# Sixteen identity products ahead of each whole K pair's first products, layers 0 and 1

## Chip, cores and metric

One core of a Trainium2 chip runs the kernel. The metric is the device time of one execution in microseconds (us); lower is better. Figures called "span" run from the first to the last instruction of one execution that was profiled.

## What is computed

Four attention layers for one token follow each other, with the weights and caches A, B, A, B. The part that matters:

```python
def _A_ref(x, k_cache, v_cache, wq, wo):          # _B_ref is the same with its own weights
    q = (x @ wq).reshape(B, Sq, Hq, Dh).transpose(0, 2, 1, 3)     # Sq = 1, Hq = 32, Dh = 192
    scores = jnp.einsum("bhqd,bhkd->bhqk", q, k) * (Dh ** -0.5)   # 8192 keys per head
    p = _softmax(scores, axis=-1)
    o = jnp.einsum("bhqk,bhkd->bhqd", p, v)
    return o.transpose(0, 2, 1, 3).reshape(B, Sq, Hq * Dh) @ wo

x = x + _A_ref(_layernorm(x), A_k_cache, A_v_cache, A_wq, A_wo)
x = x + _B_ref(_layernorm(x), B_k_cache, B_v_cache, B_wq, B_wo)
# and both once more
```

All tensors are bf16. One head's keys are 8192 x 192, so the K of two heads is 6.29 MB (6144 KB) and their V as much again. Each layer reads all 32 heads.

## The kernel before

**Tiling.** A layer works on 16 pairs of heads. K and V of a pair lie on 128 partitions with 64 partitions for each head and 128 keys on each partition. The buffer `pool` in SBUF has eight slots of 128 x 12288 bf16; one slot holds one half of a pair's keys (a "unit", 64 keys on each partition), two neighbouring slots hold a whole pair.

**Scores of a pair.** `products` (from line 725) does one unit. VectorE multiplies the K in place by the query, which is laid out as a row on every partition (line 737), in pieces along the 192 head elements: 96, 64 and 32 for the pairs that this change concerns. TensorE then adds up over the head elements: 24 products of 128 x 512 with the identity as weights accumulate in one PSUM bank of `S` (line 752 for the first, which loads the weights, and the helper at line 72 for those that keep them). Each piece is waited for by itself: 12, 8 and 4 products follow the three pieces. A second unit goes to the other bank. After both, VectorE reduces `S` to scores (line 792), `softmax` follows, and `values` (lines 822 and 849) multiplies the probabilities by V on TensorE. `gather` has VectorE collect the output (lines 873 and 875), and TensorE and ScalarE bring it into a row (lines 887 and 896). After pairs 4 and 9 the output projection of five pairs follows on TensorE (lines 715 and 688).

**Order.** The list `steps` gives the order in which every engine's instructions are written; an engine takes its own in that order. For a pair p in the middle of a layer it reads: products of one unit, products of the other, softmax, values, gather, then the same of pair p + 1. So on TensorE the products of pair p + 1 stand behind the line 887 product of pair p.

**Loads.** The list `plan` gives the order of the loads; SyncE issues them all (line 473 for K and V pairs), and each waits until its slots are free (`before`, `freed`). K's slots are free when the identity products of their unit are done, V's slots when `values` is done. In layers 0 and 1 the pairs 1 to 13 (those in `KPOS`) are loaded whole, as one transfer of 6.29 MB for K and one for V. V always goes to slots 0 and 1. K alternates between slots 2 and 3 and slots 3 and 4, so K of pair p + 1 shares one slot with K of pair p: it can be issued when the first unit of pair p is done, and `units` puts the shared slot's unit first. From pair 4 to 5 and from 9 to 10 K stays in the same two slots and waits for both units. In layers 2 and 3 the slots are handed out more freely.

**The helper `busy`** issues products of the identity with the identity, 128 x 512, into the first bank of `S`; nobody reads them. They wait until the last reduction of `S` has read that bank. The kernel uses it with 16 products at the end of layers 1 and 3, and with one to six in four other places, none of them in the middle of a layer.

Of the kernel before, what the change touches and what calls it, by code (L numbers as in the profile page):

```python
# [82 lines left out]
def build(nc, A_x, A_k, A_v, A_wq, A_wo, B_x, B_k, B_v, B_wq, B_wo, out):  # L83
# [31 lines left out]
    with ExitStack() as ctx:  # L115
# [18 lines left out]
        KPOS = {}  # L134
# [101 lines left out]
        def first_load(kind, l, p):  # L236

            n = (kind, pair(l, p))
            if l >= 2 and n in KEPT[l - 2]:
                return (l - 2, ORDER[l - 2]["pairs"].index(n[1]))  # L240
            return (l, p)
# [4 lines left out]
        def units(l, p):  # L246

            return (1, 0) if l < 2 and p in KPOS and KPOS[p] == RING else (0, 1)
# [11 lines left out]
        steps, plan, joint = [], [], set()  # L260

        def both(*ns):
            plan.extend(ns)
            steps.extend(ns)

        for l in range(NL):
            if l < 3:
                plan += [("wq", l, 0), ("wq", l, 2)][:(1, 2, 0)[l]]
                ahead_of = [{0: (0, DC)}, {0: (0, DC - 1), 2: (DC - 1, DC)}, {0: (0, 1), 2: (1, DC)}][l]
                for c in ([0, 2, 3, 1, 4] if l == 2 else range(DC)):  # L270
                    steps += [("lead", l, 0, *ahead_of[c])] if c in ahead_of else []
                    steps.append(("r", l, c))
            else:
                both(("wq", l, 0))
            for p in range(NPAIR):
                if l == 0 and p == 0:
                    plan.append(("kh", l, p))
                if l == 2 and p == 0:
                    plan += [("kp", l, p, i) for i in range(1, len(PIECE))]
                else:  # L280
                    plan += [("k", l, p, u) for u in range(2)]
                if l == 2 and p == 0:
                    steps.append(("mq", l, p, 0))
                    for i in range(1, 4):
                        steps += [("mq", l, p, i), ("rd", l, p, i - 1)]
                    steps.append(("rd", l, p, 3))
                else:
                    steps.append(("m", l, p, units(l, p)[0]))
                    if l == 2 and p == 1:
                        steps.append(("e", l, 0))  # L290
                    steps.append(("m", l, p, units(l, p)[1]))
                if p == NPAIR - 1:
                    steps.append(("v", l, p - 1))
                steps.append(("s", l, p))
                if l == 3 and p == 0:
                    both(("wq", l, 1), ("wq", l, 2))
                if p < NPAIR - 2:
                    if first_load("v", l, p) == (l, p):
                        plan += [("v", l, p, u) for u in range(2)]
                    steps.append(("v", l, p))  # L300
                    if l != 2 or p > 0:
                        steps.append(("e", l, p))
                    if p + 1 in (PAIRS_W, 2 * PAIRS_W):
                        b = (p + 1) // PAIRS_W - 1
                        steps.append(("wc", l, b))
                        both(("wo", l, b))
            for i in (p - 1, p):
                if first_load("v", l, i) == (l, i):
                    plan += [("v", l, i, u) for u in range(2)]
            plan.insert(-1 if l < 2 else -2, ("wo", l, 2))  # L310
            steps += [("busy", l, 16), ("e", l, p - 1)] if NB[l] else [("e", l, p - 1)]
            steps += [("v", l, p, 0), ("wc", l, 2)] if NB[l] else [("wc", l, 2), ("v", l, p, 0)]
            steps += [("wo", l, 2), ("v", l, p, 1), ("e", l, p)]
            if NB[l]:
                plan.append(("vq", l))
                for i in range(len(WB[l])):
                    both(("wob", l, i))
            both(("wol", l))
            if l == 3:
                both(("woe", l))  # L320
# [662 lines left out]
def bass_interleave_layers__gqa_block_cached__mha_block_cached__decode_kernel(  # L983
    nc: bass.Bass,
    A_x: bass.AP,
    A_k_cache: bass.AP,
    A_v_cache: bass.AP,
    A_wq: bass.AP,
    A_wo: bass.AP,
    B_x: bass.AP,  # L990
    B_k_cache: bass.AP,
    B_v_cache: bass.AP,
    B_wq: bass.AP,
    B_wo: bass.AP,
    out: bass.AP,
):
    build(nc, A_x, A_k_cache, A_v_cache, A_wq, A_wo, B_x, B_k_cache, B_v_cache, B_wq, B_wo, out)
# [28 lines left out]
```

## Time and profile before

| what | figure |
|---|---|
| three runs | median 1992.69 us, 1990.37 to 1992.9 |
| the profiled execution | 1993.62 us, of which the span is 1991.7 us |
| mean granted TensorE clock | 0.791 of full speed |
| busy in the span | TensorE 1274.9 us (64%), VectorE 1201.3 us (60%), ScalarE 168.5 us (8%) |
| moved by DMA | 845.99 MB, mean 425 GB/s |
| identity products over K, line 72 | x3004, 787.1 us busy, 425 ns mean |
| identity products over K, line 752 (first of a group) | x66, 38.1 us busy, idle before them 236.4 us, all of it waiting for VectorE's line 737 |
| VectorE line 737 | x408, 841.1 us busy |
| products of `busy`, lines 526 and 72 | x6 and x37, 2.7 and 8.6 us busy |
| one K pair of A from issue to landing (13 whole ones) | median 19.2 us |

"Idle before" is the time in which the engine stood still just ahead of such instructions. A product's own duration contains the way through the array, so products in a row start closer together than their durations say. The granted clock is given as a share of full speed.

### The profile page before, as it was taken

The page shows a single profiled execution, that of the slowest core. Times are in us where ns is not written, and L with a number is a line of the kernel's source. Part 1 is how long each engine was busy: PE and PEld are TensorE (multiplying, and loading weights), DVE is VectorE, ACT ScalarE, POOL GpSimd, SP SyncE. Part 2 cuts the span into 40 slices and gives each one's busy share as a digit, 9 for nine tenths or more (in the row PEclk, how much of TensorE's full clock was granted, in tenths as well). Part 3 has the DMA queues.
Part 4 walks back from the last instruction along what each step waited for, and adds up shares of the span by engine and source line. Part 5 has one row for each costly group of instructions (what it writes and reads, how often), then busy time and mean ns, then how long its engine had stood idle before and what let it go on. Part 6 is the DMA issues. An engine that isn't in the chain of part 4 may idle for free.

```text
span 1991.7 us, 12071 instructions
## 1 busy us (share of the span) xinstructions
PE 1274.9 (64%) x7747; PEld 128.0 (6%) x2611; DVE 1201.3 (60%) x858; ACT 168.5 (8%) x529; POOL 4.6 (0%) x25
## 2 busy tenths in 40 slices
PE   4475665657565656656686666666666667657558
PEld 0000000000100000010010000000002001000001
DVE  3565574667256655656756755756773666765656
ACT  1000000000100000000000000000000100000000
POOL 0000000000000000000000000000000000000000
PEclk9777777778776877777888778877787788778779
DMA  9999999999999999999999999999999999999998
GB/s 411 434 417 417 423 423 428 402 427 428 429 432 414 427 423 401 423 425 427 429 416 432 432 429 432 434 427 429 439 423 426 436 435 433 429 435 432 430 435 368
DMA packets 27240, 845.99 MB, mean 425 GB/s; under 512 B 3122, under 2 KB 3252, under 8 KB 4148
## 3 DMA queue, kind: packets, MB, share of 16 engines
q1 hardware_dynamic: 27044, 845.23, 99.3%
q8 instruction: 40, 0.66, 0.1%
q14 instruction: 12, 0.10, 0.0%
q10 hardware_dynamic: 144, 0.00, 0.0%
HBM read 845.22 MB, written 0.00 MB: 424 GB/s over the span
## 4 chain that ended last, share of the span: by engine, by line
DMA 60%; PE 22%; DVE 16%; ACT 1%; issue 0%; SPq 0%; POOL 0%; ACTq 0%
DMA pool<-in_B_k_cache_dram 26%; DMA pool<-in_A_k_cache_dram 18%; PE S L72 15%; DMA pool<-in_A_v_cache_dram 14%; DVE pool L737 13%; PE OY L72 3%; PE OY L849 2%; DMA pool<-in_B_wo_dram 2%; DVE OY L873 1%; DVE acc L875 1%; PE S L752 1%; DMA pool<-in_B_v_cache_dram 1%; DVE s_sb L792 1%; DVE pool L766 1%; ACT p_sb L807 0%
## 5 line engine op out<-in xcount | busy, mean ns | idle before, releaser
L737 DVE TENSOR_TENSOR pool<-pool,q_sb 128x3072 bf16<-128x3072 bf16 (+4 forms) x408 | 841.1, 2129 | 181.0 <-DMA pool<-in_B_k_cache_dram 98.3
L72 PE MATMUL S<-pool,ident 128*128 128x512 bf16 x3004 | 787.1, 425 | 15.8 <-DVE pool L737 13.7
L873 DVE TENSOR_TENSOR OY<-OY,small 128x1536 f32<-128x1536 f32 x60 | 106.0, 1767 | 247.5 <-PE OY L72 247.3
L72 PE MATMUL OY<-pool,p_sb 128*16 128x512 bf16 x1920 | 206.8, 519 | 0.0
L752 PE MATMUL S<-pool,ident 128*128 128x512 bf16 x66 | 38.1, 577 | 236.4 <-DVE pool L737 236.4
L887 PE MATMUL TB<-acc,small 128*33 128x192 f32 x120 | 43.9, 461 | 207.0 <-DVE acc L875 207.0
L849 PE MATMUL OY<-pool,p_sb 128*16 128x512 bf16 (+1 forms) x1216 | 144.1, 497 | 44.3 <-DMA pool<-in_A_v_cache_dram 36.2
L792 DVE TENSOR_REDUCE s_sb<-S 128x128 f32<-128x1024 f32 x63 | 77.2, 1225 | 150.5 <-PE S L72 150.5
L587 ACT ACTIVATE q_sb<-QM 64x192 bf16<-64x192 f32 x118 | 38.4, 325 | 952.5 <-PE QM L640 951.9
L875 DVE TENSOR_REDUCE acc<-OY 128x192 f32<-128x1536 f32 x60 | 105.5, 1758 | 2.0
L896 ACT ACTIVATE rows<-TB,small 1x192 bf16<-1x192 f32 x120 | 49.5, 413 | 568.8 <-PE TB L887 567.3
L807 ACT ACTIVATE p_sb<-s_sb,small 64x128 bf16<-64x128 f32 x128 | 55.7, 435 | 172.7 <-DVE small L801 171.9
L797 PE MATMUL QM<-ident,m_bf 128*64 128x64 bf16 x128 | 14.1, 217 | 82.5 <-DVE m_bf L794 82.5
L863 DVE RECIPROCAL small<-TB 33x2 f32<-33x2 f32 x64 | 11.2, 175 | 89.7 <-PE TB L822 73.3
L822 PE MATMUL TB<-small,ones 128*33 128x2 f32 x120 | 14.6, 192 | 74.1 <-ACT p_sb L807 74.1
L640 PEld LDWEIGHTS QM<-rows,one_b 1*128 1x128 bf16 x59 | 5.4, 91 | 727.8 <-issue 727.8
L849 PEld LDWEIGHTS OY<-pool,p_sb 128*16 128x16 bf16 (+1 forms) x1216 | 35.3, 107 | 195.2 <-issue 141.7
L688 PE MATMUL OY<-pool,oT 128*1 128x320 bf16 x330 | 39.0, 414 | 2.4 <-ACT oT L718 2.2
L801 DVE TENSOR_REDUCE small<-QM 128x1 f32<-128x64 f32 x64 | 14.4, 225 | 33.2 <-PE QM L797 33.2
L887 PEld LDWEIGHTS TB<-acc,small 128*33 128x33 f32 x120 | 9.9, 128 | 306.9 <-DVE acc L875 306.9
L752 PEld LDWEIGHTS S<-pool,ident 128*128 128x128 bf16 x66 | 6.8, 103 | 273.5 <-DVE pool L737 272.4
L807 ACT ACTIVATION_READ_ACCUMULATOR p_sb<-s_sb,small 64x1 f32 x128 | 23.3, 182 | 0.0
(87 smaller groups left out, 248.5 us busy)
## 6 DMA issues: line engine op xcount, KB each, us to landing
pool<-in_B_v_cache_dram SPq DMA_DIRECT2D x28, 6144.0 KB, 27.4
pool<-in_A_v_cache_dram SPq DMA_DIRECT2D x27, 6144.0 KB, 24.0
pool<-in_B_k_cache_dram SPq DMA_DIRECT2D x27, 6144.0 KB, 21.4
pool<-in_A_k_cache_dram SPq DMA_DIRECT2D x35, 3072.0 KB, 19.9
pool<-in_A_k_cache_dram SPq DMA_DIRECT2D x13, 6144.0 KB, 19.2
pool<-in_A_v_cache_dram SPq DMA_DIRECT2D x10, 3072.0 KB, 14.3
pool<-in_B_k_cache_dram SPq DMA_DIRECT2D x10, 3072.0 KB, 18.7
pool<-in_A_wo_dram SPq DMA_DIRECT2D x6, 2400.0 KB, 18.3
```

The source lines that it names most:

```text
L72: return t.add_instruction(mybir.InstMatmult(name=t.bass.get_next_instruction_name(), engine=mybir.EngineType.PE, ins=[t.lower_ap(rhs), t. ...
L587: lambda a, h=h, r=r, f=f: a.activation(q_sb[i][r, :], QM[r, h * DH:(h + 1) * DH], ACT.Copy, scale=f),
L688: e = PE.op(lambda t, i=i, h=h, f=l < 3 and n[2] == 0 and i == 0, fin=n == last_row and i == k - 1: t.matmul(YR[32 * h:32 * h + 1, :], lhs ...
L737: e = DV.op(lambda v, d0=d0, QD=QD, kin=kin, kout=kout, n=n: v.tensor_tensor(kout[:, :, d0:d0 + QD], kin[:, :, d0:d0 + QD], q_sb[qi][:, d0 ...
L752: t.matmul(S[:, :], lhsT=ident[:], rhs=k3[:, :, d0:d0 + R], start=d0 == 0, stop=fin)),
L792: lambda v: v.tensor_reduce(s[:], S_[:].rearrange("p (j r) -> p j r", r=R), AX.X, ALU.add),
L807: ev_p[p] = AC.op(lambda a, h=h, r=r: a.activation(p_sb[par][r, :, h], s[r, :], ACT.Exp, bias=negm[par][r, 0:1], accum_out=l_col[par][r, h ...
L849: t.matmul(o, lhsT=x, rhs=y, start=f, stop=fin) if c == 0 else
L873: e = DV.op(lambda v: v.tensor_tensor(o3, o3, pick[:, 0:VK].unsqueeze(2).broadcast_to([P, VK, DH]), ALU.mult), bank=Ou)
L875: e = DV.op(lambda v: v.tensor_reduce(acc[:], O.rearrange("p (i d) -> p d i", d=DH), AX.X, ALU.add), e, bank=Ou)
L887: e = PE.op(lambda t: t.matmul(TB[64:97, C_O:C_O + DH], lhsT=half33, rhs=acc[:], start=True, stop=True), bank=TBu)
L896: last["TO"] = last["row_written"] = AC.op(lambda a, h=h: a.activation(orow[:, o0 + h * DH:o0 + (h + 1) * DH], TB[64 + 32 * h:65 + 32 * h, ...
```

## The change

For each of the pairs 1 to 13 in layers 0 and 1, the step `("busy", l, 16)` is written just ahead of the products of the pair's first unit.

```diff
@@ -285,6 +285,8 @@
                         steps += [("mq", l, p, i), ("rd", l, p, i - 1)]
                     steps.append(("rd", l, p, 3))
                 else:
+                    if l < 2 and p in KPOS:
+                        steps.append(("busy", l, 16))
                     steps.append(("m", l, p, units(l, p)[0]))
                     if l == 2 and p == 1:
                         steps.append(("e", l, 0))
```

The step calls this function, which is unchanged:

```python
        def busy(n):

            PE.wait(ev_const, last["S"][0])
            for i in range(n):
                PE.op(lambda t, i=i: (
                    t.matmul(SP_[0][:, :], lhsT=ident[:], rhs=ident[:].unsqueeze(1).broadcast_to([P, 4, P]), start=True, stop=True)
                    if i == 0 else
                    matmul_held(t, SP_[0][:, :], ident[:], ident[:].unsqueeze(1).broadcast_to([P, 4, P]), True, True)),
                    signal=False, bank=Su[0])
```

## The prediction

> **What bounds the kernel now.** I began with the page's forty slices: how busy the DMA engines are, what they move, and TensorE's clock.
>
> ```profile
> PEclk9777777778776877777888778877787788778779
> GB/s 411 434 417 417 423 423 428 402 427 428 429 432 414 427 423 401 423 425 427 429 416 432 432 429 432 434 427 429 439 423 426 436 435 433 429 435 432 430 435 368
> ```
>
> The transfers run all the time, but the first half of the span has slices of 401 to 417 GB/s, the second nearly none. The table by stage says how much that is. Its rows are two stretches of layers 0 and 1 (from the landing of K of pair 1 to that of pair 13), then one of layer 2 and one of layer 3. The last three columns are granted clock, busy share of the DMA engines and GB/s.
>
> ```profile
> 66.96:437.86 370.90, 229.87 (x1326) 18.81 (x378) 224.88 (x144) 29.84 (x98) 0.00 (x0) 0.76 0.99 419
> 580.48:952.11 371.63, 229.50 (x1346) 20.41 (x398) 224.89 (x144) 30.27 (x99) 0.00 (x0) 0.77 0.99 421
> 1093.88:1500.00 406.12, 268.05 (x1477) 20.36 (x403) 259.91 (x191) 32.31 (x106) 0.00 (x0) 0.79 1.00 431
> 1560.00:1940.00 380.00, 245.68 (x1461) 21.69 (x434) 242.97 (x142) 32.52 (x107) 0.00 (x0) 0.78 1.00 432
> ```
>
> No engine but DMA is near full, so the kernel is bound by its loads, and layers 0 and 1 load some 2.6% below the pace that layers 2 and 3 hold. At 432 GB/s a pair (12.58 MB) takes 29.13 us, and the twelve pairs with two output weights of 2.46 MB (5.69 us each) take 12 x 29.13 + 2 x 5.69 = 360.9 us. The rows have 370.9 and 371.6: **20.7 us** in all are lost there.
>
> The chain of waits, in order of time (start, length, what), shows where. First comes a pair with a short turn, then one with a long one.
>
> ```profile
> 251.76 3.37 DVE pool L737
> 255.78 6.09 PE S L72 x23
> 261.89 19.17 DMA pool<-in_A_k_cache_dram
> ...
> 347.87 3.37 DVE pool L737
> 351.89 7.51 PE S L72 x23
> 359.43 19.22 DMA pool<-in_A_k_cache_dram
> ```
>
> K lands, VectorE multiplies its first piece, TensorE sums up the first unit, and only then is the next K issued: 10.1 us after the landing in one pair, 11.6 us in the other. Read off in the same way for all pairs, the 20 that free the next K with their first unit fall into groups: seven issue it 10.1 to 10.4 us after the landing, and the next K lands 29.08 to 29.66 us after this one (mean 29.37); eleven issue it after 11.2 to 11.6 us, and the next lands 29.47 to 31.07 us after (mean 30.30); two lie between, at 29.06 and 29.48. A later issue makes a longer period, some 0.8 us for each us, and the shortest period is that of the bytes. At the late issues the transfers run dry: V of the pair takes 14.6 us at that pace behind its K, whose data ends before the landing is reported.
>
> Why is TensorE early or late? Its first product starts 3.41 us after the landing in all 26 pairs, when VectorE has the first piece; and in all 26 the granted clock at that moment is 0.50. It rises during the unit, sooner or later. The two stretches by time of the products of `S` alone, from pair 6 (after length, sum and the three engines: granted clock):
>
> ```profile
> 226.00:230.00 4.00, 4.00 (x11) 0.00 (x0) 0.00 (x0) 0.50 0.91 393
> 231.00:235.00 4.00, 4.00 (x20) 0.00 (x0) 0.00 (x0) 1.00 1.06 406
> ```
>
> Each stretch is 4 us: some ten products at half clock, some twenty at full, or 0.43 and 0.215 us each.
>
> **The change part by part.** It removes nothing and moves no transfer in SyncE's order. It adds 26 x 16 = 416 products and 26 weight loads on TensorE. The nearest row is the use at the end of layer 1 (the first product with its weight load, then 15):
>
> ```profile
> 1013.27 0.39 PE L526 MATMUL S<-ident 128*128 128x512 bf16 x1
> ...
> 1013.50 3.40 PE L72 MATMUL S<-ident 128*128 128x512 bf16 x15
> ```
>
> That is 3.63 us at full clock, and by the 0.43 us above 16 x 0.43 = 6.9 us at half. In TensorE's order they stand behind the line 887 product of the pair before. How long before the landing of K that ends decides everything. An early pair and a late one:
>
> ```profile
> 375.65 0.51 PE L887 MATMUL TB<-acc,small 128*33 128x192 f32 x2 [3.66 <-DVE acc L875]
> 378.67 13.30 DVE L737 TENSOR_TENSOR pool<-pool,q_sb 128x6144 bf16<-128x6144 bf16 x6 [3.07 <-DMA pool<-in_A_k_cache_dram]
> 382.08 0.61 PE L752 MATMUL S<-pool,ident 128*128 128x512 bf16 x1 [5.92 <-DVE pool L737]
> ```
>
> ```profile
> 251.00 0.80 PE L887 MATMUL TB<-acc,small 128*33 128x192 f32 x2 [3.65 <-DVE acc L875]
> 251.76 12.17 DVE L737 TENSOR_TENSOR pool<-pool,q_sb 128x6144 bf16<-128x6144 bf16 x5 [0.82 <-DMA pool<-in_A_k_cache_dram]
> 255.18 0.61 PE L752 MATMUL S<-pool,ident 128*128 128x512 bf16 x1 [3.37 <-DVE pool L737]
> ```
>
> In the first, TensorE idles for 5.92 us up to its first product, in the second for 3.4. Of the 26 pairs, 18 are early (TensorE free 1.3 to 6.1 us before the landing), 8 late (1.0 us before to 0.12 after). What stands behind the sixteen in TensorE's order are the products of this pair, on which hang the next K's issue, softmax and V's slots.
>
> *When does the clock rise?* Its changes in the rows lie on a grid: it falls at 216.95 us and rises at 230.6, four steps of 3.41 us. It rises after a step that was nearly full of products and falls after one under about half full. Sixteen products in a row, 5 to 6.9 us, nearly always fill one step. Free at t, TensorE gets full clock between t + 2.7 and t + 6.1; the sixteen end between t + 4.8 and t + 6.5 (6 cold and 10 warm ones, or 14 and 2). The Trainium skill, "TensorE: Matmul & The Clock Gate", Part 1, says the same: a free-running window of about 3.4 us that one busy window opens and an idle one closes. The steps of 3.41 us in this trace agree.
>
> *Early pairs.* The sixteen end at about the time of the first piece and TensorE begins warm. The unit then ends at 3.41 + 12 x 0.215 = 5.99, + 8 x 0.215 = 7.71, + 4 x 0.215 = 8.57, + 0.2 us for the way out and the issue: 8.8 us after the landing, where it was 10.1 to 11.6. That issue is early enough for the period to become that of the bytes. The excess over 29.13 us in the 12 early pairs that free the next K by one unit is 10.7 us of the 20.7. **-10.7 us.** Bounds: all of it, or half if the clock falls back in half of them.
>
> *Pairs 4 and 9*, whose next K waits for both units (16 to 16.6 us after the landing): their four periods exceed the bytes' by 5.9 us. The second unit is held by VectorE, 13.3 us for six pieces, so only up to 1.4 us each is to be had. **-3 us**, between 0 and -5.9.
>
> *Late pairs.* The sixteen hold TensorE until 4.5 to 6.2 us after the landing, past the 3.41 us. From there 24 x 0.215 + 0.2 = 5.4 us: an issue at 9.9 to 11.6 us, mean 10.75, where it was 10.4. At 0.8 us for each us that is 8 x 0.35 x 0.8 = **+2.2 us**; between a gain of 4 us, which is all the excess that these pairs have, and +9 us, if all eight end at 11.6. What is late behind them is V's slot, by as much; V is issued 21.7 to 25.4 us after the landing of K today, and the next K lands 29 us after it or later.
>
> The weight loads (0.10 us) lie ahead of the products on an idle engine: nothing; without that cover 26 x 0.10 = 2.6 us. VectorE's product and reductions share no bank with the sixteen, since those wait for the last reduction of `S`, long done by then.
>
> Sum: -10.7 - 3 + 2.2 = -11.5 us on a span of 1991.7, so 1980.2 and, with the 1.9 us outside of it, 1982.1 for this execution. That execution is 0.9 us above the median, so **1981 us**. Layers 2 and 3 load at their pace whenever they begin, so the gain should reach the end.
>
> A rule that speaks against it is in the Trainium skill, "DMA: Bandwidth & Descriptors", Specifications: HBM gives one core about 358 GB/s. By it nothing could be won, since the loads would already be above their ceiling and the time would stay 1992. The rows of 431 and 432 GB/s do not bear it out; its place is in the second rival.
>
> **Rivals.** *Part of the gain.* The sixteen shift what follows, so more pairs become late; then half of the gain goes: 1987 us. For it: a shorter period by itself brings the landing nearer to line 887. Against: 18 of 26 have 1.3 us or more.
>
> *Nothing.* Either the landing is set by the slowest of the sixteen DMA engines, which is never idle, or the clock falls again before the first product. Time 1992, within 4 us. For the first: the DMA share is already 0.99. Against both: the periods follow the issue, and S products lift the clock in every pair.
>
> *Slower.* The sixteen run wholly at half clock and block. 6.9 us starting later than 3.5 us before the landing pass the first piece, and an issue at t + 6.9 + 5.4 is later than today's 10.1 to 11.6 once t is after -2.2 to -0.7. With the eight late pairs 2 us worse each, 16 us, and 9 us from early ones turned late, less half the gain of the others, it is some 20 - 6 = 14 us: 2006. For it: eight pairs are beyond that point today. Against: the clock must rise within 6.1 us.
>
> **How the numbers follow.** The forecast has 0.54 (its own range 1973 to 1986), half the gain 0.15, nothing 0.13, slower 0.18. The 1973 is all of the 20 us; the upper end takes in the two middle cases and a small loss: 1972 to 1996. A measurement of this kernel tells about 0.2% (4 us) from no change, so faster 0.70, same 0.13, slower 0.17.
>
> **What would show it.** Right: the granted clock at the first product of whole pairs is 1.00, the next K is issued 8.8 us after the landing, and the two stretches run at 428 GB/s or more, some 363 to 366 us long. Wrong: line 752 begins later than 3.41 us after the landing in half the pairs, waiting for nothing but its own queue; or it begins warm and early and the periods stay at 30 us, which would leave the gain in the slowest DMA engine.

## The result, and the profile after

Six runs of the changed kernel have a median of 1980.34 us (1977.8 to 1982.49), six of the kernel before on the same chip 1992.7 us (1990.37 to 1993.51): a ratio of **0.9938** (95% interval 0.9925 to 0.9951), 12.4 us. A second measurement on another occasion gave 0.9925 (0.9903 to 0.9947). The profiled execution of the changed kernel took 1982.49 us with a span of 1980.7 us, 11.0 us less than before. Its lines stand two higher, so line 737 of before is 739 here, 752 is 754 and 887 is 889.

From the page: the clock and the transfers in 40 slices, then two groups of instructions (busy time, mean, idle time before them).

```profile
PEclk9788887888688897878887877778787878778779
GB/s 413 428 435 423 427 431 431 432 429 429 436 428 432 428 417 436 430 409 429 438 387 435 429 430 431 429 432 433 432 428 428 437 431 433 432 433 431 433 432 365
...
L72 PE MATMUL S<-ident 128*128 128x512 bf16 x427 | 137.9, 493 | 0.0
...
L754 PE MATMUL S<-pool,ident 128*128 128x512 bf16 x66 | 33.7, 510 | 116.8 <-DVE pool L739 116.7
```

The first half of the span now loads at nearly the pace of the second, but for slices 15, 18 and 21. The unread products cost TensorE 129 us more of busy time (137.9 against 8.6), and nearly all of it is time in which it had stood still before line 754 (116.8 us, 236.4 before).

The table by stage, for the same four stretches as before (to the landing of pair 13, and one each of layers 2 and 3):

```profile
66.89:429.63 362.74, 264.40 (x1504) 19.83 (x390) 224.90 (x145) 29.66 (x98) 0.00 (x0) 0.85 1.00 430
572.15:937.59 365.44, 268.09 (x1530) 21.64 (x410) 224.88 (x144) 30.24 (x99) 0.00 (x0) 0.84 1.00 427
...
1080.00:1490.00 410.00, 270.43 (x1507) 20.39 (x409) 261.75 (x194) 33.25 (x110) 0.00 (x0) 0.80 1.00 431
1550.00:1930.00 380.00, 246.21 (x1462) 21.70 (x433) 242.97 (x141) 32.26 (x106) 0.00 (x0) 0.78 1.00 432
```

The two stretches took 370.9 and 371.6 us and now take 362.7 and 365.4: 14.4 us won of the 20.7 that lay above the bytes' time, with the granted clock at 0.85 and 0.84 instead of 0.76 and 0.77. The chain of waits shows one turn of it:

```profile
95.97 3.37 DVE pool L739
99.78 4.98 PE S L72 x23
104.77 21.50 DMA pool<-in_A_k_cache_dram
```

The 23 products that took 6.1 to 7.6 us in the chain of before take 4.98, and the next K is issued 8.80 us after the landing. That K then takes 21.50 us to land instead of some 19. Six of the nine K issued at 8.80 us land 20.3 us later: they wait longer in a queue that still has work, and come 29.06 or 29.07 us after the K before them. The turn shown is one of three that a fetch of instructions delayed as well (last section). A turn of a late pair, from the timeline of TensorE (K lands at 371.50 us):

```profile
370.16 0.51 PE L889 MATMUL TB<-acc,small 128*33 128x192 f32 x2 [3.65 <-DVE acc L877]
370.61 0.61 PE L528 MATMUL S<-ident 128*128 128x512 bf16 x1
371.01 4.87 PE L72 MATMUL S<-ident 128*128 128x512 bf16 x15
375.72 0.38 PE L754 MATMUL S<-pool,ident 128*128 128x512 bf16 x1
```

TensorE was free 0.83 us before the landing, the sixteen took 5.1 us, and the first product of K came 4.21 us after the landing instead of 3.41. It is warm, so the next K is still issued after 9.59 us.

### The profile page after: what moved, and what is told of

Same layout as the page of the kernel before. It is cut to its first block, busy times and chain, and to the rows that moved or that the text cites. A ratio compares the mean times of both kernels' runs of the same rounds, so it can differ in the third digit from the quotient of the medians.

```text
span 1980.7 us, 12513 instructions
## 1 busy us (share of the span) xinstructions
PE 1363.3 (69%) x8163; PEld 131.4 (7%) x2637; DVE 1201.2 (61%) x858; ACT 168.3 (8%) x529; POOL 4.6 (0%) x25
## 4 chain that ended last, share of the span: by engine, by line
DMA 55%; PE 23%; DVE 20%; ACT 1%; issue 0%; SPq 0%; POOL 0%; ACTq 0%
DMA pool<-in_B_k_cache_dram 23%; DMA pool<-in_A_k_cache_dram 17%; PE S L72 15%; DVE pool L739 15%; DMA pool<-in_A_v_cache_dram 12%; PE OY L72 3%; PE OY L851 2%; DMA pool<-in_B_wo_dram 2%; DVE OY L875 1%; DVE acc L877 1%; DVE s_sb L794 1%; DMA pool<-in_B_v_cache_dram 1%; PE S L754 1%; ACT p_sb L809 1%; PE OY L690 1%; DVE pool L768 1%
## 5 line engine op out<-in xcount | busy, mean ns | idle before, releaser
L72 PE MATMUL S<-pool,ident 128*128 128x512 bf16 x3004 | 748.4, 409 | 31.4 <-DVE pool L739 29.3
L72 PE MATMUL OY<-pool,p_sb 128*16 128x512 bf16 x1920 | 199.9, 504 | 0.0
L72 PE MATMUL S<-ident 128*128 128x512 bf16 x427 | 137.9, 493 | 0.0
L754 PE MATMUL S<-pool,ident 128*128 128x512 bf16 x66 | 33.7, 510 | 116.8 <-DVE pool L739 116.7
L824 PE MATMUL TB<-small,ones 128*33 128x2 f32 x120 | 14.4, 190 | 74.1 <-ACT p_sb L809 74.1
L803 DVE TENSOR_REDUCE small<-QM 128x1 f32<-128x64 f32 x64 | 14.4, 225 | 30.2 <-PE QM L799 30.2
```

What stands on the lines that cost most here:

```text
L72: return t.add_instruction(mybir.InstMatmult(name=t.bass.get_next_instruction_name(), engine=mybir.EngineType.PE, ins=[t.lower_ap(rhs), t. ...
L754: t.matmul(S[:, :], lhsT=ident[:], rhs=k3[:, :, d0:d0 + R], start=d0 == 0, stop=fin)),
```

## Experiments

Eleven kernels, the first eight of them (e1 to e8) in the table. The counts are of the 26 whole pairs and their first product of K; issue and period are means over the 20 pairs that free the next K by one unit:

| kernel | ratio to before (95%) | warm at first product | first product later than 3.6 us | mean K issue after landing | mean period | the two stretches |
|---|---|---|---|---|---|---|
| before | 1 | 0 of 26 | 0 | 10.96 us | 29.87 us | 370.9, 371.6 us |
| the change (16) | 0.9938 (0.9925 to 0.9951) | 22 | 10 | 9.67 | 29.44 | 362.7, 365.4 |
| e1, narrow | 1.0006 (0.9995 to 1.0017) | 0 | 0 | 10.73 | 30.13 | 372.5, 372.1 |
| e2, 8 | 0.9985 (0.9967 to 1.0003) | 6 | 0 | 10.48 | 29.95 | 372.5, 368.6 |
| e3, 12 | 0.9934 (0.9918 to 0.9951) | 24 | 4 | 9.23 | 29.27 | 363.7, 361.8 |
| e4, 24 | 1.0008 (0.9998 to 1.0017) | 25 | 23 | 10.50 | 29.99 | 369.9, 370.5 |
| e5, hold | 1.0075 (1.0048 to 1.0102) | 26 | 20 | 12.35 | 30.75 | 376.8, 381.3 |
| e6, layer 0 | 0.9956 (0.9939 to 0.9973) | 13 | 5 | 10.19 | 29.66 | 363.6, 370.7 |
| e7, all layers | 0.9934 (0.9909 to 0.9959) | 24 | 10 | 9.43 | 29.23 | 361.7, 362.6 |
| e8, 8 and 8 | 0.9971 (0.9956 to 0.9986) | 12 | 1 | 10.46 | 29.69 | 367.7, 367.0 |

The period goes with the issue, not with the number of warm pairs: 24, 25 and 26 warm pairs stand beside 29.27, 29.99 and 30.75 us. Small steps in it say little: two profiles of the same kernel differ by 0.1 us (29.44 and 29.32 us for sixteen products), and e1 has a period 0.26 us above that of before with an issue 0.23 us earlier. The turns of all 13 profiles together show more. In the 115 with an issue within 10.0 us the median period is 29.07 us, in the 76 from 10.0 to 11.0 us it is 29.59, in the 41 from 11.5 us on 30.79. So an issue is early enough at some 10 us, and an earlier one wins nothing more.

### e1: narrow products

```diff
-                        steps.append(("busy", l, 16))
+                        steps.append(("narrow", l, 16))
...
+                    t.matmul(SP_[0][:, 0:1], lhsT=ident[:], rhs=ident[:, 0:1], start=True, stop=True)
+                    if i == 0 else
+                    matmul_held(t, SP_[0][:, 0:1], ident[:], ident[:, 0:1], True, True)),
```

> Sixteen products of 128 x 1 in place of those of 128 x 512, in the same places, read by nobody as well. Theory (full clock at the first product makes the next K's issue early): sixteen narrow ones take about 1 us and do not fill a step of 3.41 us, so the granted clock at the first product stays 0.50, the next K is issued 10.1 to 11.6 us after the landing and the time is that of before, 1992 us within 3. Rival (the gain comes from anything else that the step brings: the wait on the last reduction, the weights being loaded already, other timing): about 1981 us.

Measured 1994.58 us against 1991.99 us. Two lines of its TensorE timeline with the first product of that pair, and its two stretches:

```profile
219.21 0.51 PE L72 MATMUL S<-ident 128*128 128x1 bf16 x15
225.90 0.61 PE L764 MATMUL S<-pool,ident 128*128 128x512 bf16 x1 [6.18 <-DVE pool L749]
```

```profile
67.07:439.60 372.53, 226.39 (x1518) 19.54 (x390) 224.89 (x145) 29.84 (x98) 0.00 (x0) 0.77 0.99 418
582.76:954.83 372.07, 231.25 (x1538) 21.57 (x410) 224.90 (x145) 30.28 (x99) 0.00 (x0) 0.76 0.99 419
```

The same instructions in the same places, but half a microsecond of them: the first product still lasts 0.61 us, as at half clock, and the gain is gone. So it is the work of the sixteen that counts, and neither their wait nor the loaded weights.

### e2, e3, e4: how many

```diff
-                        steps.append(("busy", l, 16))
+                        steps.append(("busy", l, 8))      # e3: 12, e4: 24
```

> Eight products in place of sixteen. Theory: 3.4 us at half clock fill a step only when they happen to lie on it, so the clock at the first product is full in less than half of the pairs and about a third to a half of the gain is left: 1985 to 1989 us. Rival (the number does not matter, only that TensorE is touched): 1981 us.

> Twelve products in place of sixteen. Theory with its cost term (late pairs are held by the sixteen): 12 x 0.43 = 5.2 us at half clock still fill a step in most pairs, and TensorE is free for the late pairs 0.9 to 1.7 us sooner: 1977 to 1980 us, not slower than with sixteen. Rival (the hold costs nothing, and every product less loses full clock): 1983 to 1986 us.

> Twenty-four products in place of sixteen. Theory with its cost term: 8 x 0.215 = 1.7 us more ahead of every pair; with TensorE free 0.7 to 3 us ahead of the landing they end 3.5 to 7.5 us after it, past the first piece (3.41 us) in most pairs, so the next K is issued 9 to 12.9 us after the landing although the clock is full in all of them: 1986 to 1996 us. Rival (a warm clock is worth more than a late start): 1981 us or less.

Measured 1989.13, 1978.96 and 1993.16 us beside 1991.99 of before. The last two lie inside what the theory gave, the first at the upper end of its range, and its interval (0.9967 to 1.0003) does not tell it from no change. Eight warm only 6 of 26 pairs; in 15 of the other 20 the clock did not rise before K's first product, in 5 it rose and fell again. Twelve warm 24 and hold 4. Twenty-four warm 25 and win nothing, which the timeline of e4 explains (K lands at 250.88 us):

```profile
249.84 7.33 PE L72 MATMUL S<-ident 128*128 128x512 bf16 x23
...
250.88 12.17 DVE L739 TENSOR_TENSOR pool<-pool,q_sb 128x6144 bf16<-128x6144 bf16 x5 [2.27 <-DMA pool<-in_A_k_cache_dram]
...
257.01 0.38 PE L754 MATMUL S<-pool,ident 128*128 128x512 bf16 x1
```

The first product is warm (0.38 us, not 0.61) and comes 6.13 us after the landing instead of 3.41. The two effects cancel: a full clock with late issues loads no faster than a half clock did, as the stretches say (twelve, then twenty-four):

```profile
66.84:430.51 363.67, 261.51 (x1463) 20.21 (x390) 224.92 (x144) 29.80 (x98) 0.00 (x0) 0.83 1.00 429
572.22:933.97 361.75, 259.07 (x1482) 22.10 (x410) 224.90 (x144) 30.24 (x99) 0.00 (x0) 0.84 1.00 431
```

```profile
66.99:436.87 369.88, 284.70 (x1595) 20.17 (x390) 224.90 (x144) 29.80 (x98) 0.00 (x0) 0.85 1.00 422
578.58:949.12 370.54, 288.79 (x1625) 22.20 (x410) 224.89 (x144) 29.82 (x98) 0.00 (x0) 0.85 0.99 420
```

### e5: a warm clock with a late issue

```diff
                 for c, QD in enumerate(cuts):
                     PE.wait(chunks[c])
+                    if l < 2 and p in KPOS and c == 2 and u == units(l, p)[0]:
+                        for i in range(10):
+                            PE.op(lambda t: matmul_held(t, SP_[1 - u][:, :], ident[:], ident[:].unsqueeze(1).broadcast_to([P, 4, P]), True, True),
+                                  signal=False, bank=Su[1 - u], holds=ident)
```

> The changed kernel, with ten more unread identity products inside the first unit of each of the 26 pairs, behind its second piece and ahead of its last four products. The clock stays as warm as in the changed kernel, and the second unit waits for VectorE anyway, but the end of the first unit, and with it the next K's issue, comes 10 x 0.215 = 2.15 us later: about 10.9 us after the landing. Theory (the gain is the early issue): most of it is lost, 1987 to 1993 us, and the stretches of layers 0 and 1 run at 420 to 424 GB/s. Rival (the gain is in a warm clock for what follows, such as values): 1980 to 1983 us.

Measured 2009.55 us beside 1995.48: worse than both, 17 us above the range that the theory gave (3 of them belong to the occasion, since before took 1992.7 us where the range came from). The direction speaks for it: with all 26 pairs warm, the late issue takes away more than the whole gain. The size does not, and the chain of waits shows why (from one gather to the next, with the lines of that kernel):

```profile
126.22 0.85 PE TB L893 x2
127.07 0.54 PE S L528
127.61 5.31 PE S L72 x15
132.92 0.22 PE S L758
133.14 12.32 PE S L72 x57
145.48 1.24 DVE s_sb L798
...
153.25 1.78 DVE OY L879
155.05 1.77 DVE acc L881
156.82 0.04 issue
156.86 0.85 PE TB L893 x2
```

There is no DMA in it any more. TensorE's own order has become the bound: gather's product, the sixteen, both units with the ten, softmax, values, the collecting on VectorE, gather's product again, 30.64 us from 126.22 to 156.86. I had added 2.15 us to an issue of 8.8 us; the pairs became late one after the other, and the issue came after 12.35 us on average. The same lines give the changed kernel's loop: 30.64 less 2.15 is 28.5 us, only 0.6 us below the 29.13 us of the bytes. By the same count twenty-four (8 x 0.215 = 1.7 us more) make 30.2 us, and e4's mean period was 29.99. That is an estimate from two rows; the loop gets shorter wherever values runs warm.

### e6 and e7: which layers

```diff
-                    if l < 2 and p in KPOS:
+                    if l < 1 and p in KPOS:                       # e6
+                    if p in KPOS and (l, p) != (2, 1):            # e7
```

> The sixteen products in layer 0 alone. Theory: each layer gains by itself. The stretch of layer 0 was 8.2 us shorter in the changed kernel, that of layer 1 6.2 us, and some 3 us were given back where layer 1 hands over to layer 2. With layer 0 alone the 8.2 us should arrive, since what is given back belongs to the end of layer 1: 1984 to 1986 us. If a part is given back at each end of a layer: 1986 to 1989 us.

> The sixteen products ahead of pairs 1 to 13 in layers 2 and 3 as well (all but pair 1 of layer 2). Theory: these layers load at 431 and 432 GB/s with the clock at 0.78, nothing runs dry there, so a warm clock has nothing to win: 1979 to 1983 us, as with two layers. Rival (a TensorE at full clock is worth something by itself): 1968 to 1974 us. If the sixteen hold late pairs there too: 1983 to 1988 us.

e6 took 1985.91 us and e7 1980.89 us, where before took 1995.48 us, 3 us more than where the ranges came from; by ratio e7 (0.9934) gains what the change does (0.9938). In e6 the stretch of layer 0 is 363.6 us as in the changed kernel and that of layer 1 370.7 us as before, so each layer gains by itself. In e7 the layers 2 and 3 load no faster although their clock rises from 0.80 and 0.78:

```profile
1080.00:1490.00 410.00, 303.88 (x1676) 22.00 (x423) 263.16 (x195) 34.06 (x112) 0.00 (x0) 0.82 1.00 429
1550.00:1930.00 380.00, 281.85 (x1662) 22.21 (x445) 242.72 (x141) 32.25 (x106) 0.00 (x0) 0.86 1.00 432
```

TensorE's speed by itself shows no gain here; it pays where a load waits for it.

### e8: eight ahead of gather's product, eight behind

```diff
-                        steps.append(("busy", l, 16))
+                        steps.append(("busy", l, 8))
...
+                    if l < 2 and p + 1 in KPOS:
+                        steps.append(("busy", l, 8))
                     if l != 2 or p > 0:
                         steps.append(("e", l, p))
```

> Eight of the sixteen ahead of gather's product (line 889 in the changed kernel), in the 3.65 us in which VectorE collects the output, eight behind it. Theory with its cost term: the first eight are free, TensorE is through some 2 us sooner, so the late pairs are no longer held, and the clock rises as before: 1976 to 1980 us. If eight and eight with a gap between do not fill a step, the clock at the first product stays at half in many pairs: 1983 to 1989 us.

Measured 1988.13 us: the time of the second case and its cold first products, but not its reason. Three rows from the table by stretch, for the pair whose K lands at 280.47 us; clock third from the end:

```profile
275.00:280.00 5.00, 1.80 (x8) 0.00 (x0) 0.00 (x0) 0.82 (x2) 0.00 (x0) 0.97 1.05 452
280.47:283.80 3.33, 0.00 (x0) 0.00 (x0) 3.33 (x2) 0.00 (x0) 0.00 (x0) 0.50 1.06 458
283.90:287.00 3.10, 3.10 (x8) 0.09 (x1) 3.10 (x2) 0.00 (x0) 0.00 (x0) 0.50 1.06 460
```

TensorE was fully warm and done with the second eight at 276.8 us, stood still for 7.09 us, and began K's products at half clock. So eight and eight did lift the clock: in 13 of the 14 pairs that began cold it was full when the second eight ended and fell in the 3.3 to 9.2 us up to K's first product. Being through early is as bad as being cold: only 12 of 26 pairs began warm.

### e9, e10, e11: sixteen, twelve, and twelve with six behind the projections

```diff
-                        steps.append(("busy", l, 16))                               # e9
+                        steps.append(("busy", l, 12))                               # e10
+                        steps.append(("busy", l, 6 if p % PAIRS_W == 0 else 12))    # e11
```

> The changed kernel itself, beside twelve products on the same chip. Theory with its cost term: in the profiled run the sixteen held 10 of 26 pairs beyond 3.6 us after the landing, twelve held 4 of 26 and left 24 warm, so sixteen should be 1 to 3 us slower than twelve. Rival (the hold is covered, the two numbers are alike): within 1 us.

> Twelve products, as before, beside sixteen on the same chip. Theory: 1 to 3 us faster than sixteen, ratio to before 0.992 to 0.9935. Rival: equal within 1 us.

> Twelve products, but six ahead of pairs 5 and 10, where the projection of five pairs on TensorE stands ahead of them. TensorE is through there from 1.9 us before to 0.2 us after the landing in the profiled run of twelve, with a clock already full or rising from the projection's own products. Theory: six end in time and the clock stays up from the projection: equal to twelve or up to 1.5 us faster. Rival (six do not keep a step half full, the clock falls in these four pairs): 1 to 3 us slower than twelve.

Medians 1979.38, 1978.32 and 1976.95 us beside 1993.84 of before; ratios 0.9925 (0.9903 to 0.9947), 0.992 (0.9899 to 0.9941) and 0.9916 (0.9895 to 0.9937). The order is the one expected, but the differences are within the intervals: these runs do not tell the three apart. Their profiles hold 11, 4 and 4 pairs beyond 3.6 us and begin 24, 22 and 20 warm.

## Why the prediction was right

**The place of the loss** was right: the next K's issue. e2 to e5 move that issue by another number of products and by a hold inside the unit, and the mean period follows it from 29.27 us at 9.23 us (e3) to 30.75 us at 12.35 us (e5), about 0.5 us for each us; I had read 0.8 from the pairs of one profile. e4 and e5 do not move the issue alone, since they also make TensorE's own loop longer than the bytes' time. What was lost before also shows in the packets: added up, the 16 DMA engines stood idle for a mean of 7.7 us in the two stretches before, for 0.8 us after the change (good to about 1 us), and packets that took over 2.0 us cost another 6.7 us less (last section). Together that is 13.6 of the 14.4 us won. The signs set down ahead came only in part: one stretch runs at 430 GB/s and the other at 427 where 428 was asked, and 9 of the 20 issues come at 8.8 us.

**Early pairs** came out as computed where the clock held: 8.80 us was forecast as 8.8, and the clock at the first product is full in 22 of the 26 pairs. In the other four (pairs 1 and 5 of both layers) it had risen and fallen again: TensorE was free 3.0 to 5.6 us before the landing, and through with the sixteen 2.6 to 4.4 us before K's first product. In a fifth, pair 6 of layer 1, the sixteen ended 3.7 us before that product, the clock fell 0.8 us into the unit, and the issue came after 10.49 us. e8 shows the same loss in half of its pairs. The 12 early pairs that free the next K by one unit won 7.1 us, where 10.7 were forecast.

**Late pairs** are held as described, but less: TensorE was through with the sixteen 3.9 to 4.5 us after the landing in the ordinary ones, where 4.5 to 6.2 was forecast, and the issue came at 9.1 to 9.8 us instead of 9.9 to 11.6. The exception is behind the projection of pairs 5 to 9 in layer 1. The timeline there, K landing at 847.63 us:

```profile
847.29 1.99 PE L707 MATMUL OY<-ones,pool 1*64 1x1 f32 x20 [0.53 <-ACT pool L703]
...
849.61 6.19 PE L72 MATMUL S<-ident 128*128 128x512 bf16 x15
...
855.64 0.38 PE L754 MATMUL S<-pool,ident 128*128 128x512 bf16 x1
...
861.01 0.33 SPq L475 DMA_DIRECT2D pool<-in_B_k_cache_dram  x1
```

The small products of the projection end only after the landing, the sixteen follow at half clock, and the issue comes 13.38 us after the landing. The next pair is late for it too (11.13 us). This is the mechanism of the rival "slower" in one place of 26; the two turns lie 2.6 us above the bytes' time. With twenty-four products (e4) it took the whole gain. The eight pairs that were late before won 1.5 us, where a loss of 2.2 was forecast. One reading in that term was off as well: their issue had a mean of 10.56 us, not 10.4, and at 0.8 us for each us its upper bound would be some 7 us and not 9.

**Pairs 4 and 9** were undersized: -3 us forecast, with -5.9 as the bound. Their four periods fell from 36.4, 37.3, 36.1 and 35.4 us to 34.8 to 34.9, that is by 5.8 us, to the time of the bytes. Their issue came only 0.6 to 1.3 us sooner, as forecast (at most 1.4), so what was too small is the price for each us. The other pairs gave 8.5 us in all, where -10.7 + 2.2 was forecast. That agreement is luck: the early pairs gave 3.6 us less than forecast and the late ones 3.7 us more.

**"The gain should reach the end"** was only partly so in the profile: 14.4 us were won in the two stretches and 11.0 us in the span. The rest of the execution, from pair 13 of layer 1 to the end, took 1039.6 us before and 1043.1 us after. These are the ends of a scatter over all 13 profiled executions, but not of one without order: the four with sixteen products ahead of the pairs of layer 1 (the change, e5, e7, e9) have 1042.2 to 1043.1 us, the nine others 1039.6 to 1041.3. The difference is there by the first V of layer 2, which lands 102.5 to 102.8 us after K of pair 13 in these four and 99.1 to 101.1 us after it in the nine. So with sixteen some 2 us seem to be given back at the handover to layer 2, where slice 21 fell to 387 GB/s; twenty-four products (e4, 1040.8) do not show it, and why stays open. The medians differ by 12.4 us where 11.5 was forecast; that this is so close owes something to what pairs 4 and 9 won beyond the forecast and what was given back.

**The rivals.** "Nothing" falls with the result, but both of its halves are seen in places: a landing set by the slowest DMA engine in the last section, a clock that falls again in e8. "Part of the gain" (1987 us) lies outside the interval of the ratio. The rule of the Trainium skill that was weighed, "DMA: Bandwidth & Descriptors", Specifications, some 358 GB/s for one core, does not set a ceiling here: the row divides a stack's rate by two cores, this kernel runs on one, and a whole stretch of e3 loaded at 431 GB/s. The window of the Trainium skill's "TensorE: Matmul & The Clock Gate", Part 1, agrees with what e2, e3 and e8 show: a full window ahead warms, 7.09 us of idling cools. The page speaks of an idle window that closes it; in the trace of before, the steps of 3.41 us ahead of the 114 falls were busy for a median of 0.22 of their length and for up to 0.71, so a window need not be quite idle.

## What to carry to other kernels

Where loads are the bound, ask which instruction frees the next load's buffer and how fast that one piece of work runs; an engine that is busy for two thirds of the span can still be what the queue waits for at every turn. Work that nobody reads can buy a full clock for such a piece, but it must end just before that piece starts: too few products leave the clock low, too early ones let it fall, too many stand in the way, and from 8 to 24 products, 3.4 us of full-clock work, the gain goes from 3 us to 13 and back to nothing. Before adding it, add up the engine's own loop: here some 28.5 us (the estimate at e5) under a bound of 29.13.

## What had not been expected

**A queue that runs dry costs more than its idle time.** A transfer of a whole pair consists of packets of 49152 bytes, eight for each DMA engine, and the median packet took 1.815 us. Where a K was issued at the last moment, most of its first packets took 2.0 to 3.4 us each. In the part of the span up to pair 13 of layer 1, packets over 2.0 us number 328 of 7069 before, 150 after the change, 100 with twelve products and 385 in e5; of the 328, 239 start within 3 us of the issue of a K. What they took beyond the median is 11.9, 5.3, 3.2 and 17.9 us for each engine: the change wins 6.7 us by it, about as much as by the idle time.

**A fetch of instructions can delay a landing.** The queues on the page after the change include

```profile
q8 instruction: 42, 0.69, 0.1%
```

where it was 40 before. The K that follows the chain's turn shown above was issued in time (8.80 us) and yet landed 30.33 us after its predecessor: a fetch of 16 KB began at 117.1 us, one DMA engine's next packet took 2.3 us, and that engine finished its share of K at 125.83 us when the middle one of the sixteen had at 123.24. K's landing, at 126.27 us, is that of the last engine. It is not one place: over the 13 profiles there are 115 turns with an issue within 10.0 us, and of the 65 in which a fetch began between 2 us before K's landing and the next landing, 22 took more than 29.4 us; of the 50 without one, two did (29.41 us). This is read from what falls together in the traces; no run moved a fetch. Read so, the 6.3 us by which the two stretches still exceed the bytes' time are 2.6 us in three turns with a fetch, 2.6 us in the two behind the projection and 1.5 us in three whose clock had fallen.
